# Denominators, scalings and the low halves of O: from VectorE to GpSimd

## The chip, the cores and the metric

The kernel runs on one core of one Trainium2 chip. The metric is the device time of one execution in microseconds. A core has five engines that work side by side, each in the order of its own queue: TensorE (PE, with its weight loads as PEld), VectorE (DVE), ScalarE (ACT), GpSimd (POOL) and SyncE (SP), which here issues the DMAs.

## The reference

Two attention branches A and B of the same form read the same x (2048 tokens, 640 channels, 32 heads of 20 channels); their outputs are mixed by a gate of each token. Each branch goes through four segments of 512 tokens with a memory M and its normalizer z:

```
for s in range(4):                      # qs, ks, vs: this segment's 512 tokens
    logits = qs @ ks.T * 20**-0.5 + mask          # mask: -1e9 where key > query
    a_dot  = softmax(logits) @ vs
    num    = phi(qs) @ M                           # phi(t) = t+1 if t>0 else exp(t)
    den    = phi(qs) @ z + 1e-6
    o      = g * num / den + (1 - g) * a_dot       # g = sigmoid(beta), one per head
    M, z   = M + phi(ks).T @ vs, z + phi(ks).sum
branch = concat(o) @ wo
out = gate * branch_A + (1 - gate) * branch_B      # gate = sigmoid(sum(x * gate_w))
```

(The mask of the reference is `ar[:, None] < ar[None, :]`, so a query sees the keys up to its own place.)

## The kernel before

The work is cut into eight batches t = 0..7: branch t % 2 of segment t // 2. A batch has eight groups u of four heads each; i = 8 t + u counts the 64 groups.

Products of x with the weights, and of O with wo, are done in three parts: each operand is split into hi (rounded by ScalarE) and lo (the difference). The lo halves of the weights come from GpSimd (`stage`, L541 and L516, 128x640, in four early cases from VectorE), those of O from `o_turn` (L948). Most matmuls use one half of the array, 64 rows of weights, so that two streams of them run side by side.

For each group the kernel makes the scores twice. The S units (L1240) give the scores with a query to a partition; VectorE adds the mask `tri` and takes each row's maximum in one operation (L1227, on a PSUM bank). The maxima are split and turned and sent into the rows of `qst`, so that the T units (L1330) give the scores turned and with their maximum taken off. ScalarE takes the exponential (L1322), GpSimd clears what lies past the diagonal (L1323), and TensorE multiplies with v in `pv_unit` (L1352), four heads at once, with a column of ones that gives the softmax's denominator.

What `pv_unit` and `mem_unit` (L827: phi(q) with M and z) leave in a PSUM bank goes through `weighed`. There are 112 calls: 64 for the attention (`which` = 0) and 48 for the memory (`which` = 1; the two batches of the first segment have no memory):

1. VectorE turns the bank in blocks of 32 (L934), after which each partition is a token and the denominators stand in column DH = 20 of each head.
2. `weight` makes the 16 factors of each partition: denominator times 1 / gate, then the reciprocal (L856). The product is L855 for the attention and L852 for the memory, where 1e-6 is added in the same instruction. Both run on VectorE, with both operands (the turned tile and the gates `gq`) in SBUF.
3. `pair` multiplies the 20 columns of each head by their factor (L878 into the tiles Z of the batch, L881 in place) and, where both attention and memory exist, adds the two (L886). `anyof` gives each of these to VectorE or GpSimd, to whichever has the smaller load.

When a Z tile has all its parts, `o_turn` turns it back (L952, 40 tiles in all), ScalarE makes hi (L947) and VectorE or GpSimd makes lo (L948). The q and k products (80 of them) are emptied by `hi_lo_out` and `hi_lo_phi` (L686 to L719).

The order of every engine's queue is written beforehand, by a planner inside the program. `put(engine, duration, instruction, then, prio)` puts a piece of work into a queue by priority, with a duration that stands in the code; the planner's clock goes on with the matmuls that it lays down, and an event `then` releases the next piece. What is written in this way is fixed when the kernel is built: on the chip each engine works its queue from front to back, and waits where an operand isn't there. The table `RULES` sets, for each of the 64 groups, in what succession S and T units are laid among the other products, how long the group's stretch is, and at which load of VectorE small units are held back. A line of it reads "order, span, calm, lag, room".

The names that count below: `fw` is the tile of 16 factors, `gqd` and `gqm` are the gates for attention and memory, `row` are the 42 large SBUF tiles that are used for everything, `mx` the row maxima, `bank` the eight PSUM banks.

Of the kernel before, what the change touches and what calls it, by code (L numbers as in the profile page):

```python
# [12 lines left out]
F32 = mybir.dt.float32  # L13
# [24 lines left out]
def r32(ap):  # L38
    return ap.bitcast(F32)
# [3 lines left out]
def tile_gated_mix_infini_attn(  # L43
# [44 lines left out]


    RULES = {  # L90
        0: "TTSTSTSTSS 1.0 2.63 0.33 6",
        1: "TSTSTSTSTS 1.0 2.38 0.46 6",
        2: "TSTTSSTSTS 1.0 2.38 0.46 4",
        3: "TSTTSSTSTS 1.0 2.38 0.42 4",
        4: "TTSSTTSSTS 1.0 2.93 0.42 4",
        5: "TSTTSSTSTS 0.996 2.28 0.34 6",
        6: "TSTTSSTSTS 0.954 2.96 0.46 8",
        7: "TSTTSSTSTS 0.964 2.58 0.34 8",
        8: "TSTSTSTSTS 1.0 2.21 0.33 8",
        9: "TTSTSTSTSS 0.95 2.38 0.36 6",  # L100
        10: "TSTSTSTSTS 1.0 2.12 0.46 6",
        11: "SSSTSTSTTT 1.0 2.12 0.46 3",
        12: "TSTTSSTSTS 1.021 2.11 0.33 4",
        13: "TSTSTSTSTS 1.0 2.38 0.33 6",
        14: "TSSTTSSTTS 1.025 2.36 0.36 6",
        15: "STSTSTSTST 1.067 2.36 0.36 6",
        16: "TSTSTSTSTS 1.029 2.38 0.33 6",
        17: "SSSTSTSTTT 1.029 1.79 0.33 6",
        18: "STTSSTTSST 1.029 2.14 0.46 6",
        19: "TSTSTSTSTS 1.0 1.84 0.31 6",  # L110
        20: "SSTSTSTSTT 1.0 1.84 0.31 6",
        21: "TSTSTSTSTS 1.0 2.38 0.36 6",
        22: "TTSTSTSTSS 1.0 2.38 0.33 6",
        23: "TTTSTSTSSS 1.012 2.38 0.33 3",
        24: "TSTSTSTSTS 0.989 2.38 0.42 4",
        25: "TTTSTSTSSS 0.993 2.38 0.33 6",
        26: "STSTSTSTST 0.989 2.38 0.33 6",
        27: "SSTSTSTSTT 0.96 3.85 0.46 6",
        28: "SSSTSTSTTT 0.922 3.85 0.46 6",
        29: "TSTSTSTSTS 0.987 2.38 0.34 6",  # L120
        30: "SSSTSTSTTT 1.014 2.38 0.36 6",
        31: "TSTTSSTSTS 1.08 2.38 0.36 6",
        32: "TTSTSTSTSS 1.0 1.82 0.36 6",
        33: "TTSSTTSSTS 1.0 2.38 0.33 6",
        34: "TSTSTSTSTS 1.0 2.38 0.34 6",
        35: "TTTSTSTSSS 1.0 1.93 0.34 6",
        36: "TTSTSTSTSS 1.033 2.93 0.33 4",
        37: "STTSSTTSST 0.932 1.97 0.33 6",
        38: "TSTSTSTSTS 1.0 2.74 0.33 6",
        39: "TSTSTSTSTS 0.971 2.38 0.31 6",  # L130
        40: "TSTSTSTSTS 1.005 2.38 0.32 6",
        41: "TSTSTTSTSS 1.007 2.38 0.32 6",
        42: "TSTSTTSTSS 1.039 2.38 0.32 6",
        43: "SSTSTSTSTT 1.039 2.38 0.34 6",
        44: "TSTSTSTSTS 1.032 2.73 0.33 8",
        46: "TSTTSSTSTS 1.032 2.73 0.31 8",
        47: "TSTSTSTSTS 0.953 1.56 0.3 6",
        48: "SSTSTSTSTT 0.953 1.56 0.46 6",
        49: "SSTSTSTSTT 0.915 1.56 0.36 6",
        50: "SSTSTSTSTT 0.915 1.56 0.42 6",  # L140
        51: "TSTSTSTSTS 0.991 2.93 0.33 6",
        52: "TSTSTSTSTS 1.0 1.87 0.33 6",
        54: "TSTSTSTSTS 0.992 2.38 0.33 6",
        55: "TTSTSTSTSS 1.0 2.38 0.33 6",
        56: "TSTSTSTSTS 1.0 2.38 0.33 6",
        58: "STSTSTSTST 1.0 3.17 0.33 3",
        59: "TSTSTSTSTS 1.055 3.17 0.33 8",
        60: "TSTTSSTSTS 0.988 2.38 0.36 6",
        61: "TSTSTSTSTS 0.976 2.38 0.33 6",
    }  # L150
    rule = {}
    DONE = {"A": 0.14, "D": 0.12, "G": 0.1, "S": 0.0}
# [33 lines left out]
    def put(e, dur, emit, then=None, prio=5, more=0.0):  # L186
        heapq.heappush(ready[e], (prio, next(seq), dur, emit, then, more))
        load[e] += dur
        start_next(e)
# [14 lines left out]
    def anyof(prio, then, **ways):  # L204

        e = min(ways, key=lambda e: load[e] + ways[e][0] + FAVOUR * (e == "D"))
        put(e, *ways[e], then, prio)
# [636 lines left out]
    def weighed(t, u, b, z, which):  # L844

        z4 = z.rearrange("p (a e) -> p a e", e=32)
        first = which == 1 or t < 2

        def weight():
            w = sb.tile([P, 16], F32, tag="fw", name=f"fw{which}_{t}_{u}", bufs=4)  # L850
            if which:
                nc.vector.scalar_tensor_tensor(  # L852
                    out=w, in0=z4[:, :, DH], scalar=1e-6, in1=gq[t][1][:, u, :], op0=ALU.add, op1=ALU.mult)
            else:
                nc.vector.tensor_tensor(out=w, in0=z4[:, :, DH], in1=gq[t][0][:, u, :], op=ALU.mult)  # L855
            nc.vector.reciprocal(w, w)  # L856
            return w

        def places(fn):
            todo = [k for k, _, _ in ZP[u] if (t, k) not in Z]  # L860
            left = then_all(len(todo) + 1, fn)
            for k in todo:
                Z[t, k] = None
                z_left[t, k] = (1 if t < 2 else 2) * sum(k == k2 for p in ZP for k2, _, _ in p)
                big.want((F32,), lambda tile, k=k: (Z.__setitem__((t, k), tile), left()), prio=1)
            left()

        def when_placed(fn):
            if all(Z[t, k] is not None for k, _, _ in ZP[u]):
                fn()  # L870
            else:
                at(clk[0] + 0.2, lambda: when_placed(fn))

        def scale(e, w):
            wb = w[:, :, None].to_broadcast([P, 16, DH])
            for k, e0, e1 in ZP[u]:
                dst = Z[t, k].rearrange("p (a e) -> p a e", e=32)[:, :, DH * u + e0 - 32 * k:DH * u + e1 - 32 * k]
                e.tensor_tensor(out=dst, in0=z4[:, :, e0:e1], in1=wb[:, :, e0:e1], op=ALU.mult)  # L878

        def scale_own(e, w):  # L880
            e.tensor_tensor(out=z4[:, :, :DH], in0=z4[:, :, :DH], in1=w[:, :, None].to_broadcast([P, 16, DH]), op=ALU.mult)  # L881

        def add(e):
            for k, e0, e1 in ZP[u]:
                dst = Z[t, k].rearrange("p (a e) -> p a e", e=32)[:, :, DH * u + e0 - 32 * k:DH * u + e1 - 32 * k]
                e.tensor_tensor(out=dst, in0=dst, in1=z4[:, :, e0:e1], op=ALU.add)  # L886

        def end():
            big.give(z)
            if which:  # L890
                mem_done.add((t, u))
            else:
                fin_done.add(i8)
                if all(8 * t + j in fin_done for j in range(8)):
                    gq_store.give(gq.pop(t))
            for k, _, _ in ZP[u]:
                z_left[t, k] -= 1
                if not z_left[t, k]:
                    big.want((F32,), lambda o, k=k: o_turn(t, k, o), prio=2)

        i8 = 8 * t + u
        n = len(ZP[u])
        D1, G1 = 0.11 * n + 0.42, 0.14 * n + 0.55

        def turned():
            bank.give(b)
            when_gates(lambda: put("D", 0.39, lambda: got_w.append(weight()), lambda: when_placed(go), prio=2))

        def when_gates(fn):
            if t in gq:  # L910
                fn()
            else:
                at(clk[0] + 0.2, lambda: when_gates(fn))

        got_w = []

        def go():
            w = got_w[0]
            if first:
                pair(D1, G1, lambda e: scale(e, w), end, 3)  # L920
            else:
                pair(0.56, 0.69, lambda e: scale_own(e, w), plus, 3)

        def plus():
            if (t, u) in mem_done:
                pair(D1, G1, add, end, 3)
            else:
                at(clk[0] + 0.2, plus)

        def pair(d, g, fn, then, prio):  # L930
            anyof(prio, then, D=(d, lambda: fn(nc.vector)), G=(g, lambda: fn(nc.gpsimd)))

        places(lambda: None)
        put("D", 0.635, lambda: nc.vector.transpose(out=z, in_=b), turned, prio=2)  # L934

    def o_turn(t, k, o):

        def turned():
            big.give(Z.pop((t, k)))
            big.want((F32R, F32R), halves, prio=2)  # L940

        def halves(hi, lo):
            def end():
                big.give(o)
                OTs[t, k] = (hi, lo)

            put("A", 0.535, lambda: nc.scalar.copy(hi, o), lambda: anyof(  # L947
                2, end, **{x: (c, lambda e=e: e.tensor_tensor(out=lo, in0=o, in1=r32(hi), op=ALU.subtract))  # L948
                           for x, c, e in (("D", 0.78, nc.vector), ("G", 1.255, nc.gpsimd))}), prio=2)

        z = Z[t, k]
        put("D", 0.63, lambda: nc.vector.transpose(out=o, in_=z), turned, prio=2)  # L952
# [676 lines left out]
```

## Time and profile before

| what | value |
|---|---|
| median of three runs | 1041.88 us (1040.1 to 1042.78) |
| the profiled execution | 1042.72 us, of which 1040.7 us lie between first and last instruction |
| TensorE clock granted | 0.998 on the mean |
| instructions | 29678 |
| busy, share of the span | PE 98%, PEld 81%, VectorE 79%, GpSimd 68%, ScalarE 60% |
| DMA | 217.65 MB, mean 209 GB/s |

A group in the profile is a line with engine, operation, tiles out<-in and shape; then the count, the busy time in us, the mean of one in ns, and the idle time of the engine just before these instructions with what ended it. The chain that ended last goes back from the last instruction, at each step to what released it or to the instruction before it on its engine. A wait is read "who <- for whom: us in total, times, longest".

### The profile page before, as it was taken

What the parts mean: (1) busy time and instruction counts of PE and PEld (TensorE: products, weight loads), DVE (VectorE), ACT (ScalarE), POOL (GpSimd) and SP (SyncE); (2) the same over time, 40 slices, a digit from 0 to 9 for tenths busy, and PEclk for the clock granted to TensorE, in tenths of its full rate; (3) what the DMA queues carried; (4) which work ended last, traced back from release to release, by engine and by line L of the source; (5) the groups of instructions that cost most, each with busy time, mean ns of one, the idle gap of its engine ahead of it and who ended that gap; (6) DMA issues with size and microseconds to landing.
All of it is one profiled execution on the core that took longest, in us unless ns stands there. A gap on an engine that the chain in (4) does not pass through costs nothing.

```text
span 1040.7 us, 29678 instructions
## 1 busy us (share of the span) xinstructions
PE 1023.1 (98%) x10610; PEld 843.0 (81%) x10610; DVE 824.3 (79%) x2814; ACT 629.1 (60%) x1286; POOL 703.1 (68%) x1230
## 2 busy tenths in 40 slices
PE   9999999999999999999999999999999999999998
PEld 7888787887888778888787888888778888687885
DVE  5797999768787789886979769987687966988864
ACT  6276667566565566665865556566575655666672
POOL 6266757667476686866857667686786766767584
PEclk9999999999999999999999999999999999999999
DMA  8998999758456677755856667675576666758631
GB/s 269 292 305 260 305 306 326 209 164 248 136 187 197 178 251 207 237 154 168 256 152 183 192 179 238 205 231 167 164 229 181 220 190 192 240 170 237 160 119 62
DMA packets 138595, 217.65 MB, mean 209 GB/s; under 512 B 12816, under 2 KB 48912, under 8 KB 138384
## 3 DMA queue, kind: packets, MB, share of 16 engines
q1 hardware_dynamic: 138448, 215.76, 68.1%
q8 instruction: 84, 1.38, 0.6%
q14 instruction: 63, 0.52, 0.2%
HBM read 141.26 MB, written 83.23 MB: 216 GB/s over the span
## 4 chain that ended last, share of the span: by engine, by line
PE 80%; DVE 9%; DMA 5%; ACT 2%; issue 2%; POOL 1%; SPq 0%; DVEq 0%; ACTq 0%
PE bank L734 47%; PE bank L1352 12%; PE bank L1330 7%; PE bank L1240 7%; PE bank L827 3%; PE bank L997 2%; DVE bank L1227 2%; DMA kst<-kd 1%; DVE row L934 1%; DVE row L703 1%; DMA qst<-qd 1%; DMA wst<-in_a_wk_dram 1%; PE bank L958 1%; DMA row<-in_xT_dram 1%; DMA kd<-row 0%
## 5 line engine op out<-in xcount | busy, mean ns | idle before, releaser
L1227 DVE CUSTOM_DVE_ANT_0 bank<-bank,tri 128x384 f32<-128x384 f32 (+3 forms) x1024 | 473.7, 514 | 77.6 <-PE bank L1240 60.6
L734 PE MATMUL bank<-row,wh 64*128 64x512 f32 x2308 | 520.6, 405 | 0.1
L1322 ACT ACTIVATE p<-bank 128x512 f32<-128x512 f32 x540 | 296.4, 602 | 160.2 <-PE bank L1330 123.9
L734 PEld LDWEIGHTS bank<-row,wh 64*128 64x128 f32 x2308 | 325.3, 186 | 19.2 <-PE bank L734 2.5
L734 PE MATMUL bank<-row,wl 64*128 64x512 f32 x1154 | 303.2, 400 | 0.0
L1323 POOL TENSOR_SCALAR_AFFINE_SELECT p<-p 128x256 f32<-128x256 f32 (+1 forms) x540 | 200.7, 383 | 102.8 <-ACT p L1322 95.0
L541 POOL TENSOR_TENSOR wl<-wst,wh 128x640 fp32r<-128x640 f32 x115 | 180.2, 1570 | 36.5 <-ACT wh L539 36.0
L734 PE MATMUL bank<-wvh,row 64*128 64x320 f32 x1280 | 194.4, 315 | 0.1
L1240 PE MATMUL bank<-kst,qst 60*128 60x384 f32 (+3 forms) x1024 | 181.0, 325 | 5.7 <-DVE mx L1227 2.4
L734 PEld LDWEIGHTS bank<-row,wl 64*128 64x128 f32 x1154 | 175.8, 185 | 6.8 <-issue 1.0
L1330 PE MATMUL bank<-qst,kst 62*128 62x384 f32 (+3 forms) x1024 | 177.6, 324 | 2.7 <-DVE row L693 1.2
L734 PEld LDWEIGHTS bank<-wvh,row 64*128 64x128 f32 x1280 | 159.6, 185 | 5.3 <-PE bank L734 1.1
L1240 PEld LDWEIGHTS bank<-kst,qst 60*128 60x128 f32 x1024 | 129.8, 186 | 21.8 <-DVE mx L1227 6.1
L1227 DVE DVE_READ_ACCUMULATOR2_ANT mx<- 128x1 f32 x1024 | 143.2, 140 | 0.1
L1330 PEld LDWEIGHTS bank<-qst,kst 62*128 62x128 f32 x1024 | 127.7, 185 | 18.0 <-issue 4.0
L934 DVE STREAM_TRANSPOSE row<-bank 128x512 f32<-128x512 f32 x112 | 77.9, 705 | 74.9 <-PE bank L1352 52.2
L1352 PE MATMUL bank<-p,vst 128*32 128x128 f32 (+3 forms) x1824 | 137.1, 421 | 0.0
L1352 PEld LDWEIGHTS bank<-p,vst 128*32 128x32 f32 x1824 | 56.6, 110 | 82.8 <-issue 57.4
L734 PE MATMUL bank<-wvl,row 64*128 64x320 f32 x640 | 110.6, 314 | 0.0
L539 ACT CAST wh<-wst 128x640 fp32r<-128x640 f32 x119 | 86.0, 738 | 32.9 <-PE bank L734 17.1
L734 PEld LDWEIGHTS bank<-wvl,row 64*128 64x128 f32 x640 | 87.8, 186 | 0.7 <-issue 0.2
L827 PE MATMUL bank<-row,mall 64*128 64x512 f32 x192 | 84.0, 606 | 1.1 <-DVE mx L1227 1.0
(99 smaller groups left out, 1296.8 us busy)
## 6 DMA issues: line engine op xcount, KB each, us to landing
qd<-row SPq DMA_DIRECT2D x120, 256.0 KB
kd<-row SPq DMA_DIRECT2D x120, 256.0 KB
qst<-qd SPq DMA_DIRECT2D x128, 240.0 KB
kst<-kd SPq DMA_DIRECT2D x128, 240.0 KB
wst<-wop SPq DMA_DIRECT2D x40, 320.0 KB
wst<-in_a_wq_dram SPq DMA_DIRECT2D x20, 320.0 KB
wst<-in_a_wk_dram SPq DMA_DIRECT2D x20, 320.0 KB
wst<-in_b_wq_dram SPq DMA_DIRECT2D x20, 320.0 KB
```

Source lines behind the costliest of these rows:

```text
L539: put("A", 0.628, lambda: nc.scalar.copy(wh, w3), lambda: put(lo_eng, lo_cost, lambda: lo.tensor_tensor(out=wl, in0=w3, in1=r32(wh), op=AL ...
L541: lambda: lo.tensor_tensor(out=wl, in0=w3, in1=r32(wh), op=ALU.subtract), end, prio=3), prio=6)
L734: return nc.tensor.matmul(bank_of, lhsT=w[ROWS[half]], rhs=x_[ROWS[half]], start=start, stop=stop)
L827: return nc.tensor.matmul(b, lhsT=w[r], rhs=r32(pqTs[t, half_m[half]][r, :]), start=start, stop=stop)
L934: put("D", 0.635, lambda: nc.vector.transpose(out=z, in_=b), turned, prio=2)
L997: return nc.tensor.matmul(b[:, :nh * E1], lhsT=r32(pkn[ROWS[half], P * n:P * (n + 1)]), rhs=vst[ROWS[half], n, LO[m] * E1:(HI[m] + 1) * E1 ...
L1227: put("D", w / 960.0 + 0.112, lambda: nc.vector.tensor_tensor_reduce(out=sc[:, off:off + w], in0=sc[:, off:off + w], in1=tri[:, L - w:], s ...
L1240: lane_ops[half].append((cost_r(w), lambda pair=pair, qb=qb, off=off, w=w, r=r, sc=sc: nc.tensor.matmul(sc[:, off:off + w], lhsT=q[r, pair ...
L1322: put("A", 0.493, lambda: nc.scalar.activation(pt, sc, AF.Exp, scale=SCALE), lambda: (bank.give(sc), put("G", 0.137 + 0.118 * len(todo), l ...
L1323: "G", 0.137 + 0.118 * len(todo), lambda: nc.gpsimd.affine_select(out=blocks, in_=blocks, pattern=[[0, len(todo)], [1, P]], base=0, channe ...
L1330: lane_ops[half].append((cost_r(w), lambda pair=pair, kb=kb, off=off, w=w, r=r, sc=sc: nc.tensor.matmul(sc[:, off:off + w], lhsT=k[r, pair ...
L1352: nc.tensor.matmul(po[32 * j:32 * j + 32, P * kb:], lhsT=vst[:, kb, h * E1:h * E1 + 32], rhs=pts[i, n, f][0][:, off:off + w], start=(kb == ...
```

## The change

In `weighed`, the product of denominators and gates is put to GpSimd for all 112 calls; for the 48 of the memory ScalarE first adds 1e-6 into `fw`. The reciprocal stays on VectorE and is released by GpSimd's product. `pair` (scaling and adding) and the lo halves of O go to GpSimd always. `fw` gets eight buffers in place of four. The table `RULES` has other entries for nearly all groups; its form and the code that reads it are as before.

```diff
     RULES = {
-        0: "TTSTSTSTSS 1.0 2.63 0.33 6",
+        0: "TSTSTSTSTS 1.001 3.28 0.33 6",
...
         def weight():
-            w = sb.tile([P, 16], F32, tag="fw", name=f"fw{which}_{t}_{u}", bufs=4)
+            w = sb.tile([P, 16], F32, tag="fw", name=f"fw{which}_{t}_{u}", bufs=8)
+            got_w.append(w)
+
+            def gated(den):
+                put("G", 0.19, lambda: nc.gpsimd.tensor_tensor(out=w, in0=den, in1=gq[t][which][:, u, :], op=ALU.mult), lambda: put(
+                    "D", 0.18, lambda: nc.vector.reciprocal(w, w), lambda: when_placed(go), prio=2), prio=1)
+
             if which:
-                nc.vector.scalar_tensor_tensor(
-                    out=w, in0=z4[:, :, DH], scalar=1e-6, in1=gq[t][1][:, u, :], op0=ALU.add, op1=ALU.mult)
+                put("A", 0.11, lambda: nc.scalar.add(w, z4[:, :, DH], 1e-6), lambda: gated(w), prio=1)
             else:
-                nc.vector.tensor_tensor(out=w, in0=z4[:, :, DH], in1=gq[t][0][:, u, :], op=ALU.mult)
-            nc.vector.reciprocal(w, w)
-            return w
+                gated(z4[:, :, DH])
...
         def turned():
             bank.give(b)
-            when_gates(lambda: put("D", 0.39, lambda: got_w.append(weight()), lambda: when_placed(go), prio=2))
+            when_gates(weight)
...
         def pair(d, g, fn, then, prio):
-            anyof(prio, then, D=(d, lambda: fn(nc.vector)), G=(g, lambda: fn(nc.gpsimd)))
+            put("G", g, lambda: fn(nc.gpsimd), then, prio)
...
-            put("A", 0.535, lambda: nc.scalar.copy(hi, o), lambda: anyof(
-                2, end, **{x: (c, lambda e=e: e.tensor_tensor(out=lo, in0=o, in1=r32(hi), op=ALU.subtract))
-                           for x, c, e in (("D", 0.78, nc.vector), ("G", 1.255, nc.gpsimd))}), prio=2)
+            put("A", 0.535, lambda: nc.scalar.copy(hi, o), lambda: put(
+                "G", 1.255, lambda: nc.gpsimd.tensor_tensor(out=lo, in0=o, in1=r32(hi), op=ALU.subtract), end, prio=2), prio=2)
```

In the order of the built programs the instructions of each kind are as many as before, apart from these: on VectorE 112 products, 23 scalings, 3 additions and 6 differences are gone, and GpSimd has these 144 more (1379 rows in place of 1235); ScalarE has 48 more. (One q or k product is emptied in the other of its two ways.) TensorE and SyncE have the same work in another succession. Three lines fewer stand in the table, so that the line numbers are smaller by one to four: the maxima are L1226, the products L851, the reciprocals L852, the weight splits L538 and L513, the turning of Z L951.

The first place is the fifth batch (t = 4), its second memory group, on VectorE before. `ISA` with `bank,tri` is the sum with mask and the maximum of a row; `ISA` with `mx` alone reads the maximum out.

```order
L934 STREAM_TRANSPOSE row37_9834_8212<-bank6_121 128x512
L1227 ISA bank3_118,mx31_8152<-bank3_118,tri_69 128x128
L1227 ISA mx31_8152 128x1
L852 SCALAR_TENSOR_TENSOR fw1_4_1_8227<-row37_9834_8212,gqm0_139 128x16
L856 RECIPROCAL fw1_4_1_8227<-fw1_4_1_8227 128x16
L703 TENSOR_TENSOR row41_9843_8216<-bank4_119,row16_9842_8215 128x512
L1227 ISA bank2_117,mx31_8152<-bank2_117,tri_69 128x128
```

The same group on VectorE now:

```order
L934 STREAM_TRANSPOSE row41_10191_8350<-bank5_120 128x512
L690 SCALAR_TENSOR_TENSOR row7_10143_8321<-bank4_119,row7_10143_8321 128x512
L934 STREAM_TRANSPOSE row22_10197_8352<-bank2_117 128x512
L852 RECIPROCAL fw1_4_1_8362<-fw1_4_1_8362 128x16
L1226 ISA bank0_115,mx31_8112<-bank0_115,tri_69 128x512
L1226 ISA mx31_8112 128x1
L934 STREAM_TRANSPOSE row40_10239_8385<-bank6_121 128x512
L852 RECIPROCAL fw1_4_2_8377<-fw1_4_2_8377 128x16
```

And on GpSimd now, where the product of the group stands:

```order
L538 TENSOR_TENSOR wl2_132<-wst1_124,wh2_131 128x640
L948 TENSOR_TENSOR row16_10176_8340<-row0_10157_8327,row13_10175_8339 128x512
L851 TENSOR_TENSOR fw1_4_1_8362<-fw1_4_1_8362,gqm0_139 128x16
L878 TENSOR_TENSOR row21_10070_8259<-row41_10191_8350,fw1_4_1_8362 128x16x12
L878 TENSOR_TENSOR row3_10193_8351<-row41_10191_8350,fw1_4_1_8362 128x16x8
L851 TENSOR_TENSOR fw1_4_2_8377<-fw1_4_2_8377,gqm0_139 128x16
L538 TENSOR_TENSOR wl1_130<-wst0_123,wh1_129 128x640
```

The product has left VectorE's queue, and the reciprocal there, which stands ahead of a row maximum, depends on a queue of GpSimd in which a weight split and a lo half of O come first.

The second place is the end of the kernel, the last group (fw0_7_7). VectorE before:

```order
L952 STREAM_TRANSPOSE row34_19729_16369<-row22_18361_15241 128x512
L934 STREAM_TRANSPOSE row28_19743_16391<-bank0_115 128x512
L855 TENSOR_TENSOR fw0_7_7_16400<-row28_19743_16391,gqd1_140 128x16
L856 RECIPROCAL fw0_7_7_16400<-fw0_7_7_16400 128x16
L881 TENSOR_TENSOR row28_19743_16391<-row28_19743_16391,fw0_7_7_16400 128x16x20
L952 STREAM_TRANSPOSE row27_19761_16421<-row20_18711_15537 128x512
```

GpSimd now:

```order
L1322 AFFINE_SELECT p4_20167_16357<-p4_20167_16357 128x2x128
L948 TENSOR_TENSOR row2_20216_16397<-row13_20201_16385,row36_20215_16396 128x512
L538 TENSOR_TENSOR wl3_134<-wst1_124,wh3_133 128x640
L851 TENSOR_TENSOR fw0_7_7_16444<-row18_20254_16436,gqd1_140 128x16
L881 TENSOR_TENSOR row18_20254_16436<-row18_20254_16436,fw0_7_7_16444 128x16x20
L886 TENSOR_TENSOR row9_19106_15494<-row9_19106_15494,row18_20254_16436 128x16x20
```

The last product and the last scaling stand on GpSimd, behind a lo half of O and a weight split.

More of the change, by code (lines that the diff above doesn't have):

```diff
@@ L90, in tile_gated_mix_infini_attn @@
     RULES = {
-        0: "TTSTSTSTSS 1.0 2.63 0.33 6",
[L92 to L149, printed above, removed]
+        0: "TSTSTSTSTS 1.001 3.28 0.33 6",
@@ new lines, in tile_gated_mix_infini_attn @@
+        2: "SSTSTSTSTT 1.0 2.38 0.33 6",
+        3: "TSTSTSTSTS 0.982 2.66 0.31 6",
+        4: "TSTTSSTSTS 0.971 1.95 0.33 6",
+        5: "TSSTTSSTTS 0.971 1.95 0.32 6",
+        6: "TSSTTSSTTS 1.0 2.38 0.33 6",
+        7: "STTSSTTSST 1.0 1.51 0.33 6",
+        8: "TTSSTTSSTS 1.02 1.52 0.31 3",
+        9: "SSSTSTSTTT 1.0 2.38 0.31 3",
+        11: "TSTSTTSTSS 0.957 2.38 0.32 8",
+        12: "TSTSTSTSTS 0.957 1.75 0.32 8",
+        13: "TSSTTSSTTS 1.003 2.38 0.42 6",
+        14: "TTSSTTSSTS 1.0 2.38 0.33 6",
@@ new lines, in tile_gated_mix_infini_attn @@
+        15: "STSTSTSTST 1.0 2.38 0.46 6",
+        16: "TSTSTSTSTS 1.0 2.38 0.46 8",
+        17: "SSTSTSTSTT 1.019 2.38 0.33 6",
+        18: "STSTSTSTST 1.0 1.98 0.33 6",
+        19: "STTSSTTSST 1.042 1.98 0.33 6",
+        20: "TSTSTSTSTS 0.982 2.22 0.46 6",
+        21: "TSTTSSTSTS 0.982 2.94 0.46 6",
+        22: "TSTSTSTSTS 1.0 2.0 0.33 6",
+        23: "SSTSTSTSTT 1.0 2.62 0.32 6",
+        24: "TSTSTTSTSS 1.0 2.62 0.32 6",
+        25: "TSTSTTSTSS 0.972 2.62 0.46 6",
+        27: "TSTSTSTSTS 1.051 2.38 0.3 3",
@@ new lines, in tile_gated_mix_infini_attn @@
+        28: "SSTSTSTSTT 1.0 2.38 0.33 6",
+        29: "TSTSTTSTSS 0.99 2.86 0.33 6",
+        30: "STTSSTTSST 0.99 2.86 0.38 3",
+        31: "TSTTSSTSTS 0.972 2.61 0.33 6",
+        32: "TSTSTSTSTS 1.0 2.38 0.33 6",
+        33: "TSTSTSTSTS 0.972 2.38 0.33 4",
+        34: "TSTTSSTSTS 1.022 1.5 0.46 6",
+        35: "TSTSTTSTSS 1.03 1.5 0.3 4",
+        36: "TSTSTSTSTS 1.034 3.14 0.33 6",
+        37: "TSTSTTSTSS 1.025 2.38 0.33 6",
+        38: "TSTSTSTSTS 0.951 2.38 0.33 6",
+        39: "TSTSTSTSTS 1.0 2.38 0.42 6",
@@ new lines, in tile_gated_mix_infini_attn @@
+        40: "TSTTSSTSTS 1.0 2.31 0.33 6",
+        41: "STTSSTTSST 1.026 2.31 0.36 6",
+        42: "TSTSTSTSTS 0.959 1.22 0.33 6",
+        43: "TTTSTSTSSS 0.959 1.31 0.3 6",
+        44: "TSSTTSSTTS 1.0 2.9 0.33 6",
+        45: "SSTSTSTSTT 1.0 2.36 0.33 6",
+        46: "SSTSTSTSTT 1.0 1.0 0.32 6",
+        47: "TSTSTSTSTS 0.964 2.38 0.33 6",
+        48: "TSTSTSTSTS 1.0 2.33 0.33 6",
+        49: "TTSTSTSTSS 1.02 3.17 0.33 6",
+        50: "TTSTSTSTSS 1.02 3.17 0.46 6",
+        51: "TTSTSTSTSS 1.02 3.27 0.32 6",
@@ L150, in tile_gated_mix_infini_attn @@
+        52: "TSTSTSTSTS 1.037 1.97 0.33 6",
+        53: "TTSSTTSSTS 0.969 3.01 0.31 3",
+        54: "TSTSTSTSTS 0.962 2.38 0.34 6",
+        56: "SSTSTSTSTT 0.951 2.2 0.34 6",
+        57: "TSTSTSTSTS 1.0 2.38 0.38 6",
+        58: "TSTSTSTSTS 1.019 1.34 0.38 6",
+        60: "TSTSTSTSTS 1.03 2.38 0.33 8",
     }
```

## The prediction

> **What bounds the kernel now.** I read the page first (busy times and the chain that ended last), then the busy time by stretches.
>
> ```profile
> PE 1023.1 (98%) x10610; PEld 843.0 (81%) x10610; DVE 824.3 (79%) x2814; ACT 629.1 (60%) x1286; POOL 703.1 (68%) x1230
> ...
> PE 80%; DVE 9%; DMA 5%; ACT 2%; issue 2%; POOL 1%; SPq 0%; DVEq 0%; ACTq 0%
> ```
>
> ```profile
> 80.00:500.00 420.00, 416.35 (x4451) 347.12 (x4444) 340.30 (x1176) 261.40 (x539) 286.43 (x505) 1.00 0.72 221
> 500.00:1000.00 500.00, 494.96 (x5157) 405.27 (x5155) 401.58 (x1389) 303.93 (x624) 351.58 (x620) 1.00 0.66 196
> ```
>
> The columns after the length are PE, PEld, DVE, ACT and POOL. TensorE is busy all but 8.7 of the 920 us between 80 and 1000, at full clock, so the matmuls bound the kernel. But almost all of them work on one half of the array, and "busy" is the union of both halves: one half can wait without any idle time in this row. The chain says as much: only 80% of it is TensorE's, and 9% (0.09 x 1040.7 = 94 us) is VectorE's, which is 94 / 824.3 = 11% of VectorE's busy time. GpSimd has 1% (10.4 us, 1.5% of its busy time), ScalarE 2% (20.8 us, 3.3% of its).
>
> What VectorE's part looks like shows best at 510 us, in the timeline, at one of the operations that the change moves:
>
> ```profile
> 509.85 1.56 POOL L541 TENSOR_TENSOR wl<-wst,wh 128x640 fp32r<-128x640 f32 x1
> ...
> 509.94 1.49 DVE L852 SCALAR_TENSOR_TENSOR fw<-row,gqm 128x16 f32<-128x16 f32 x1
> ...
> 511.47 0.25 DVE L856 RECIPROCAL fw<-fw 128x16 f32<-128x16 f32 x1
> 511.64 0.63 DVE L703 TENSOR_TENSOR row<-bank,row 128x512 fp32r<-128x512 f32 x1
> ...
> 512.19 0.28 DVE L1227 CUSTOM_DVE_ANT_0 bank<-bank,tri 128x128 f32<-128x128 f32 x1
> ...
> 512.58 0.18 PEld L827 LDWEIGHTS bank<-row,mall 64*128 64x128 f32 x1 [1.18 <-DVE mx L1227]
> ```
>
> Sixteen columns took 1.49 us, and they ended at 511.43, just when GpSimd's split of a weight tile ended (509.85 + 1.56 = 511.41). The row maximum (L1227) stood behind it in VectorE's queue, and TensorE's weight load waited 1.18 us for that maximum. Operations with two operands in SBUF do this; the reciprocal between them, with one, does not (0.25).
>
> The Trainium skill, "SBUF — State Buffer", section "Who interferes with whom", has this as a rule: VectorE with two SBUF inputs and a GpSimd instruction that reads SBUF share one read interface, and whichever came second is blocked until the first is through. The trace agrees (1.49 us, ended by the 1.56 us split). By that rule every such wait goes with the change; by the rows alone I count only what lies above the unblocked time, which comes to the same sum below.
>
> **Part 1: what leaves VectorE.** Groups by line and form (busy us, mean ns), and for some the shortest, median and longest of one:
>
> ```profile
> L855 DVE TENSOR_TENSOR fw<-row,gqd 128x16 f32<-128x16 f32 x64 | 22.4, 350 | 0.7
> ...
> L852 DVE SCALAR_TENSOR_TENSOR fw<-row,gqm 128x16 f32<-128x16 f32 x48 | 13.4, 279 | 0.2
> ...
> L881 DVE TENSOR_TENSOR row<-row,fw 128x320 f32<-128x320 f32 x8 | 6.3, 794 | 0.1
> ...
> L878 DVE TENSOR_TENSOR row<-row,fw 128x320 f32<-128x320 f32 x7 | 5.7, 813 | 0.1
> ...
> L886 DVE TENSOR_TENSOR row<-row,row 128x320 f32<-128x320 f32 x3 | 2.8, 930 | 0.1
> L878 DVE TENSOR_TENSOR row<-row,fw 128x256 f32<-128x256 f32 x3 | 2.7, 891 | 0.0
> ...
> L878 DVE TENSOR_TENSOR row<-row,fw 128x64 f32<-128x64 f32 x3 | 2.0, 661 | 0.0
> ```
>
> ```profile
> L855 DVE TENSOR_TENSOR fw<-row,gqd x64: 160/184/1517, 70.9 to 1026.0; 128x16 f32<-128x16 f32 x64
> ...
> L852 DVE SCALAR_TENSOR_TENSOR fw<-row,gqm x48: 109/160/1494, 250.1 to 973.5; 128x16 f32<-128x16 f32 x48
> ...
> L881 DVE TENSOR_TENSOR row<-row,fw x8: 490/618/1797, 427.2 to 1027.2; 128x320 f32<-128x320 f32 x8
> ...
> L878 DVE TENSOR_TENSOR row<-row,fw x15: 304/519/1516, 110.4 to 825.3; 128x320 f32<-128x320 f32 x7, 128x64 f32<-128x64 f32 x3, 128x256 f32<-128x256 f32 x3, 128x192 f32<-128x192 f32 x1
> ...
> L856 DVE RECIPROCAL fw<-fw x112: 252/253/255, 72.1 to 1026.9; 128x16 f32<-128x16 f32 x112
> ...
> L948 DVE TENSOR_TENSOR row<-row,row x6: 681/805/1652, 114.8 to 642.4; 128x512 fp32r<-128x512 f32 x6
> ```
>
> Busy time that leaves: 22.4 + 13.4 + 6.3 + 5.7 + 2.8 + 2.7 + 2.0, about 1.5 for the two L878 forms left out, and about 5.6 for the six L948 (6 x 0.94, between their median and longest) = 62 us, 7.6% of VectorE's work. Of it, blocked time above the median or the shortest of the same shape: L855 64 x (350 - 184) = 10.6; L852 48 x (279 - 160) = 5.7; L881 8 x (794 - 490) = 2.4; L878 7 x (813 - 490) + 3 x (891 - 490) + 3 x (661 - 304) = 4.5; L886 3 x (930 - 490) = 1.3; L948 6 x (940 - 681) = 1.6. Together 26 us blocked and 36 us of plain work.
>
> How much of each lay on the path? The plain work goes at VectorE's average, 11%: 36 x 0.11 = 4 us (from 0, if other work fills the place, to twice that). Blocked time comes unannounced in an order written beforehand, so it weighs more. The chain in order of time holds 19 pieces of the moved operations; the first, the large ones and the last are:
>
> ```profile
> 71.02 1.02 DVE fw L855
> ...
> 110.36 1.33 DVE row L878 x2
> ...
> 510.08 1.37 DVE fw L852
> ...
> 775.56 1.14 DVE fw L852
> ...
> 894.20 1.39 DVE fw L855
> ...
> 901.33 0.86 DVE fw L852
> ...
> 903.39 0.08 DVE fw L852
> ```
>
> The six large pieces make 7.1 us, so at least 0.27 of the 26 lies on the chain. The ends are 11% (3 us, the average) and 92% (1.37 of the 1.49 at 510 us; 24 us). I take 0.4, near the counted pieces and a little above for the small ones: 10.4 us.
>
> **Part 2: what GpSimd and ScalarE get.** The nearest rows of the same kind:
>
> ```profile
> L881 POOL TENSOR_TENSOR row<-row,fw 128x320 f32<-128x320 f32 x40 | 29.2, 730 | 37.6 <-DVE fw L856 36.2 <-PE bank L1330 1.4
> ...
> L878 POOL TENSOR_TENSOR row<-row,fw 128x320 f32<-128x320 f32 x25 | 18.5, 741 | 10.7 <-DVE fw L856 8.8 <-DVE fw L852 2.0
> L886 POOL TENSOR_TENSOR row<-row,row 128x320 f32<-128x320 f32 x21 | 18.3, 870 | 2.6 <-DVE row L881 2.3
> ...
> L948 POOL TENSOR_TENSOR row<-row,row 128x512 fp32r<-128x512 f32 x34 | 44.1, 1298 | 21.4 <-ACT row L947 21.1
> ...
> L1252 POOL TENSOR_TENSOR mt<-mx,mt 128x16 fp32r<-128x16 f32 x64 | 15.7, 245 | 29.7 <-ACT mt L1251 29.5
> ...
> L1251 ACT CAST mt<-mx 128x16 fp32r<-128x16 f32 x64 | 13.4, 210 | 34.9 <-DVE mx L1227 34.7
> ```
>
> 112 products of denominators and gates at 0.245 = 27; 8 x 0.730 + 15 x 0.741 at most + 3 x 0.870 + 6 x 1.298 = 27. GpSimd goes from 703 to 757 us (73%), and at its 1.5% this costs 0.8 us. ScalarE gets 48 additions of 1e-6 at 0.21 = 10 us; at 3.3%, 0.3 us. The moved scalings are slower by 0.24 each (730 against 490), but what follows them (adding, turning, splitting O) is wanted a batch later, and no wait of TensorE in the trace names them.
>
> **Part 3: the new wait.** The reciprocal stays on VectorE and now waits for GpSimd's product. If that is late, the row maxima behind the reciprocal are late too. Before, the trace has no such wait; it has two like it:
>
> ```profile
> DVE row L703 <- ACT row L691: 16.5, 22, 3.4
> ...
> DVE row L952 <- POOL row L886: 3.5, 3, 1.7
> ```
>
> Spread over all 80 of L703 and all 40 of L952 these are 0.21 and 0.09 us per operation; the ends for 112 reciprocals are 0 and 0.45 us (twice the worse row, since a product can stand behind a 1.56 us split). GpSimd's hand-over is the nearer kind, so I take 0.1: 11 us of VectorE, unannounced like the blocked time, so x 0.4 = 4.5 us back (0 to 20).
>
> **Part 4: the end.** Here the waits meet:
>
> ```profile
> 1025.55 1.29 POOL L948 TENSOR_TENSOR row<-row,row 128x512 fp32r<-128x512 f32 x1 [2.25 <-ACT row L947]
> ...
> 1026.04 0.83 DVE L855 TENSOR_TENSOR fw<-row,gqd 128x16 f32<-128x16 f32 x1
> ```
>
> The product of the last group was blocked for 0.65 us (0.83 against 0.18), hidden behind matmuls. In the new order it stands on GpSimd behind that L948 and behind a weight split whose lo half the early matmuls want right after the last attention product. Hidden or not: 0 to 2.8 us (both instructions); I take 1.
>
> **Sum.** -10.4 - 4 + 0.8 + 0.3 + 4.5 + 1 = -7.8 us. The new table of places writes the whole order anew and has no price in the trace; I give it 0, with 5 either way. Against the profiled execution (1042.72, with 1040.7 of it span) this is 1034.9; that execution lies 0.84 above the median of the runs, 1041.88, and from the median it is 1034.1. I forecast 1034.
>
> **The rivals.**
> 1. *The reciprocals block VectorE.* By the same terms without part 3 the gain is 12.3; part 3 gives 112 x 0.4 = 45 us back per us of mean wait, so from 0.27 us on the kernel is no faster. For it: GpSimd works in order with 1.56 us splits, and in the new order one of them stands directly ahead of the product in 25 of 112 places; against: GpSimd's own times hardly scatter, so an order that plans them can hold. At 0.45 us: -12.3 + 20 = +8, about 1050.
> 2. *Nothing to tell.* The waits of a half of the array go to whatever is late next (a bank that ScalarE still reads, a DMA, 5% of the chain): part 1's price is the low end, 3 + 0, less 2 for parts 2 and 4 and 1 or so for part 3: about 1042. The union's 99% speaks for it, the 1.18 us weight load against.
> 3. *GpSimd still holds VectorE up.* The Trainium skill, "Perfetto Trace Analysis", section "Optimizing Scalar/DVE Operations", warns that moving work between these two engines might not help, since they share a port. As a mechanism of this kernel: 55 us more of GpSimd would block whatever VectorE keeps. But what it keeps in the steady state reads at most one tensor from SBUF, apart from the few token gates, and all 112 reciprocals took 252 to 255 ns, whatever GpSimd did; so 1041, no gain, with a small chance.
>
> That the move doesn't take place is excluded: in the order no product, scaling or addition of these lines is left on VectorE.
>
> **How the numbers follow.** A measurement of this kernel tells about 0.3%, 3 us. The forecast has 0.63 (own range 1027 to 1040; it holds the faster cases), rival 1 has 0.19, rival 2 0.14, rival 3 0.04. Faster 0.63, same 0.18, slower 0.19. The range reaches down to 1022 (blocked time at 0.7 instead of 0.4, no new wait) and up to 1046, where a part of rival 1 is left out.
>
> **What would show it.** In the new profile: VectorE near 762 us busy, no operation on it with 16 columns over 0.3 us, GpSimd near 757, ScalarE near 639; VectorE's share of the chain below 9%; waits "DVE fw <- POOL fw" of about 11 us in total. I am wrong if those waits pass 30 us, if row maxima wait behind them, or if VectorE's share falls and DMA or ScalarE takes it over one for one.

## The result, and the profile after

The changed kernel takes 1030.53 us (median of 4 runs, 1028.84 to 1031.61) against 1041.37 of the kernel before: ratio 0.9894, 95% interval 0.9874 to 0.9914, so 10.8 us or 1.1% faster. The forecast was 1034. (All ratios here, and the time of experiment 1, are formed over the undisturbed runs; one execution of experiment 1 took 3420.65 us.)

The page of the changed kernel, busy times and chain:

```profile
PE 1012.2 (98%) x10610; PEld 842.2 (82%) x10610; DVE 772.2 (75%) x2671; ACT 637.0 (62%) x1333; POOL 744.5 (72%) x1374
...
PE 77%; DMA 9%; DVE 6%; ACT 2%; POOL 2%; issue 2%; SPq 1%; DVEq 0%; POOLq 0%; ACTq 0%
```

VectorE has 52 us less, GpSimd 41 more, ScalarE 8 more. VectorE's share of the chain fell from 9% to 6%, and DMA's rose from 5% to 9%. The stretches (PE, PEld, DVE, ACT, POOL):

```profile
80.00:500.00 420.00, 417.19 (x4521) 350.18 (x4519) 320.40 (x1127) 272.26 (x571) 310.75 (x576) 1.00 0.74 226
500.00:1000.00 500.00, 495.14 (x5198) 409.30 (x5196) 380.20 (x1335) 312.46 (x660) 375.77 (x708) 1.00 0.65 194
```

TensorE's busy time hardly differs (912.3 of 920 us against 911.3), but 9719 matmuls fall into these stretches instead of 9608. So the halves of the array must wait less, which the union of their busy times cannot show.

The operations that moved, by line and form, and the wait that is new:

```profile
L852 DVE RECIPROCAL fw<-fw 128x16 f32<-128x16 f32 x112 | 26.9, 245 | 10.6 <-POOL fw L851 10.1
...
L851 POOL TENSOR_TENSOR fw<-row,gqd 128x16 f32<-128x16 f32 x64 | 14.5, 227 | 60.1 <-DVE row L934 57.7 <-DMA kst<-kd 2.1
...
L855 ACT ACTIVATE fw<-row 128x16 f32<-128x16 f32 x48 | 11.1, 232 | 22.9 <-DVE row L934 22.8
L851 POOL TENSOR_TENSOR fw<-fw,gqm 128x16 f32<-128x16 f32 x48 | 10.7, 225 | 11.6 <-ACT fw L855 11.2
```

```profile
DVE fw L852 <- POOL fw L851: 10.1, 22, 1.3
```

On GpSimd the products take 225 to 227 ns each. The reciprocals waited for them 10.1 us in all, in 22 of 112 cases.

### The profile page after: what moved, and what is told of

It is laid out like the page before. It is cut to its first block, busy times and chain, and to the rows that moved or that the text cites. A ratio compares the mean times of both kernels' runs of the same rounds, so it can differ in the third digit from the quotient of the medians.

```text
span 1029.4 us, 29770 instructions
## 1 busy us (share of the span) xinstructions
PE 1012.2 (98%) x10610; PEld 842.2 (82%) x10610; DVE 772.2 (75%) x2671; ACT 637.0 (62%) x1333; POOL 744.5 (72%) x1374
## 4 chain that ended last, share of the span: by engine, by line
PE 77%; DMA 9%; DVE 6%; ACT 2%; POOL 2%; issue 2%; SPq 1%; DVEq 0%; POOLq 0%; ACTq 0%
PE bank L731 45%; PE bank L1351 12%; PE bank L1329 6%; PE bank L1239 6%; PE bank L824 3%; PE bank L996 2%; DVE bank L1226 2%; DMA kd<-row 2%; DMA wst<-in_x_dram 1%; DVE pgt L623 1%; DMA lin<-nat 1%; DMA qd<-row 1%; DMA wst<-in_a_wk_dram 1%; PE bank L957 1%; DMA wop<-lin 1%
## 5 line engine op out<-in xcount | busy, mean ns | idle before, releaser
L1226 DVE CUSTOM_DVE_ANT_0 bank<-bank,tri 128x384 f32<-128x384 f32 (+3 forms) x1024 | 473.9, 514 | 96.7 <-PE bank L1239 75.3
L1322 POOL TENSOR_SCALAR_AFFINE_SELECT p<-p 128x256 f32<-128x256 f32 (+1 forms) x536 | 195.5, 378 | 71.9 <-ACT p L1321 62.8
L538 POOL TENSOR_TENSOR wl<-wst,wh 128x640 fp32r<-128x640 f32 x115 | 180.2, 1569 | 29.6 <-ACT wh L536 28.4
L731 PE MATMUL bank<-wvh,row 64*128 64x320 f32 x1280 | 199.0, 321 | 0.0
L1226 DVE DVE_READ_ACCUMULATOR2_ANT mx<- 128x1 f32 x1024 | 143.5, 140 | 0.1
L1351 PE MATMUL bank<-p,vst 128*32 128x256 f32 (+3 forms) x1800 | 137.3, 422 | 0.0
L1321 ACT ACTIVATE row<-bank 128x512 f32<-128x512 f32 x104 | 56.5, 605 | 39.6 <-PE bank L1329 34.5
```

What stands on the lines that cost most here:

```text
L538: lambda: lo.tensor_tensor(out=wl, in0=w3, in1=r32(wh), op=ALU.subtract), end, prio=3), prio=6)
L731: return nc.tensor.matmul(bank_of, lhsT=w[ROWS[half]], rhs=x_[ROWS[half]], start=start, stop=stop)
L1226: put("D", w / 960.0 + 0.112, lambda: nc.vector.tensor_tensor_reduce(out=sc[:, off:off + w], in0=sc[:, off:off + w], in1=tri[:, L - w:], s ...
L1321: put("A", 0.493, lambda: nc.scalar.activation(pt, sc, AF.Exp, scale=SCALE), lambda: (bank.give(sc), put("G", 0.137 + 0.118 * len(todo), l ...
L1322: "G", 0.137 + 0.118 * len(todo), lambda: nc.gpsimd.affine_select(out=blocks, in_=blocks, pattern=[[0, len(todo)], [1, P]], base=0, channe ...
L1351: nc.tensor.matmul(po[32 * j:32 * j + 32, P * kb:], lhsT=vst[:, kb, h * E1:h * E1 + 32], rhs=pts[i, n, f][0][:, off:off + w], start=(kb == ...
```

## Experiments

**1. One operand instead of two, in the order of before.**

```diff
-                nc.vector.scalar_tensor_tensor(
-                    out=w, in0=z4[:, :, DH], scalar=1e-6, in1=gq[t][1][:, u, :], op0=ALU.add, op1=ALU.mult)
+                nc.vector.tensor_scalar(w, z4[:, :, DH], 1e-6, 1.0, op0=ALU.add, op1=ALU.mult)
...
-                nc.vector.tensor_tensor(out=w, in0=z4[:, :, DH], in1=gq[t][0][:, u, :], op=ALU.mult)
+                nc.vector.tensor_scalar(w, z4[:, :, DH], 0.0, 1.0, op0=ALU.add, op1=ALU.mult)
```

> The kernel before, every engine's order unchanged, but the 112 products of denominators and gates read one SBUF tensor only (the gates are left out: times 1.0). Port theory (the gain came from VectorE operations with two SBUF operands being blocked by GpSimd): none of the 112 takes over 0.3 us any more, their 16 us of blocked time go, and at the 0.4 of the prediction the time falls by 6.5 to about 1035. Table theory (the gain came from the new succession of units): stays at 1041 within 3. Load theory (the gain came from fewer operations on VectorE): stays at 1041, since the count is the same.

Measured: 1039.78 us, ratio 0.9995 (0.9979 to 1.0012). The edit failed to remove what it was meant to remove (shortest, median and longest of one, in ns):

```profile
L854 DVE TENSOR_SCALAR fw<-row x64: 153/176/1504, 70.3 to 1025.5; 128x16 f32<-128x16 f32 x64
L852 DVE TENSOR_SCALAR fw<-row x48: 109/157/1274, 251.0 to 973.0; 128x16 f32<-128x16 f32 x48
```

Sixteen columns of one SBUF tensor are held up just as long. With means of 358 and 253 ns, 64 x (358 - 176) + 48 x (253 - 157) ns = 16 us are blocked, as much as before. So the run says nothing for or against any theory, except that two operands are not the criterion; and leaving out the gates shows no gain by itself. It needed an operation that GpSimd had not held up so far; the reciprocals were one.

**2. A reciprocal in place of each product, in the order of before.** Both products are replaced by `nc.vector.reciprocal(w, z4[:, :, DH])`; the gates and the 1e-6 are left out.

> The kernel before with the same order everywhere; each of the 112 products on VectorE is replaced by a reciprocal of the denominator, followed by the reciprocal that was there (gates left out). A reciprocal was never held up by GpSimd so far (252 to 255 ns), a sum with one SBUF operand was. Port theory: no fw operation over 0.3 us; 16 us of blocked time go, 8 us of plain work come (64 x 0.07 + 48 x 0.09), so 1041 - 6.5 + 0.9 = about 1035. Table theory and load theory: 1041 or 1042.

Measured: 1035.47 us, ratio 0.9957 (0.9936 to 0.9978), 4.5 us faster. The longest of one, and one that runs beside a weight split of GpSimd:

```profile
L854 DVE RECIPROCAL fw<-row x64: 231/249/256, 70.7 to 1017.5; 128x16 f32<-128x16 f32 x64
L852 DVE RECIPROCAL fw<-row x48: 192/211/255, 249.4 to 965.0; 128x16 f32<-128x16 f32 x48
```

```profile
508.92 1.56 POOL L541 TENSOR_TENSOR wl<-wst,wh 128x640 fp32r<-128x640 f32 x1
...
509.07 0.25 DVE L852 RECIPROCAL fw<-row 128x16 f32<-128x16 f32 x1
```

This is the place that the prediction showed with 1.49 us: the same order, 0.15 us into the split, and now 0.25 us. With the number of operations and their places unchanged, the blocked time of the products was worth 4.5 us (2.3 to 6.7 by the interval), and VectorE's share of the chain went to 5%. Experiment 1 leaves out the gates as well and gained nothing, so it is not the missing operand. Port theory's cause, the blocked time, holds for the products, though its criterion of two operands does not; the two others had 1041 or 1042.

**3. The products back on VectorE, in the order of the changed kernel.** `nc.gpsimd` becomes `nc.vector` in the one line that multiplies; places, table and every other engine's order stay.

> The changed kernel with the same order of TensorE, ScalarE and SyncE and the same table; only the 112 products are issued on VectorE instead of GpSimd, at the same place of the succession. Port theory: blocked time comes back, 16 us or a little more since GpSimd is busier, 1036 to 1040. Table theory: 1030 to 1032. Load theory: 112 x 0.17 = 19 us more plain work at 11%, 2 us: about 1033.

Measured: 1035.46 us, ratio 0.9937 (0.9915 to 0.9959), so 4.5 us of the gain are gone.

```profile
L851 DVE TENSOR_TENSOR fw<-row,gqd 128x16 f32<-128x16 f32 x64 | 17.7, 276 | 0.6
L851 DVE TENSOR_TENSOR fw<-fw,gqm 128x16 f32<-128x16 f32 x48 | 14.8, 315 | 0.8 <-ACT fw L855 0.7
```

```profile
L851 DVE TENSOR_TENSOR fw<-row,gqd x64: 111/178/1445, 74.0 to 1019.7; 128x16 f32<-128x16 f32 x64
...
L851 DVE TENSOR_TENSOR fw<-fw,gqm x48: 111/171/1557, 248.4 to 965.1; 128x16 f32<-128x16 f32 x48
```

Their medians are 178 and 171 ns, so 64 x 0.098 + 48 x 0.144 = 13 us are blocked. The time lies half a microsecond below the port theory's range and above those of the others; by itself this run does not tell blocked time from load, which the next one does.

**4. The same, but with reciprocals.** On VectorE `nc.vector.reciprocal(w, den)` stands where GpSimd had the product; the gates are left out.

> The changed kernel with the same order otherwise; each product on GpSimd is replaced by a reciprocal of the denominator on VectorE at the same place (gates left out). VectorE has 112 more operations, 27 us, none of which GpSimd can hold up. Port theory: 27 x 0.11 = 3 us less what the hand-over to GpSimd cost (4.5): 1029 to 1032, clearly below the 1035.5 with products on VectorE. Load theory: 1034 to 1036, as with the products.

Measured: 1031.37 us, ratio 0.9909 (0.9887 to 0.9931), not to be told from the changed kernel (0.9894). None of the reciprocals was held up:

```profile
L851 DVE RECIPROCAL fw<-row x64: 194/250/255, 74.1 to 1016.2; 128x16 f32<-128x16 f32 x64
...
L851 DVE RECIPROCAL fw<-fw x48: 193/243/254, 249.7 to 961.6; 128x16 f32<-128x16 f32 x48
```

```profile
PE 1014.3 (98%) x10610; PEld 841.5 (82%) x10610; DVE 790.9 (77%) x2783; ACT 637.6 (62%) x1333; POOL 722.6 (70%) x1262
...
PE 83%; DMA 7%; DVE 6%; POOL 1%; ACT 1%; issue 1%; SPq 1%; POOLq 0%; ACTq 0%; DVEq 0%
```

VectorE has as many operations as in experiment 3 and is busy for 790.9 us (798.0 there), and yet the loss is not there. So the loss of experiment 3 points to blocked time and not to load: the time lies in port theory's range and outside that of load theory. The step is likely rather than certain by this pair alone, since the runs differ by 4.1 us in the medians and 2.9 in the ratios, and their intervals overlap from 0.9915 to 0.9931; experiment 2 shows the same in the order of before. Against the changed kernel the run measures one difference, 27 us of plain work on VectorE less the hand-over to GpSimd: 0.8 us by the medians, 1.6 by the ratios. So the hand-over costs no more than the work that it saves VectorE; what each costs alone, this run does not tell.

**5. Each table with the other code.** Only the entries of `RULES` are exchanged.

> The changed code with the table of the kernel before. Table theory: 1041 or worse. Port theory: the blocked time stays away, so below 1041 even with a table chosen for another order, 1032 to 1039.

> The code of before with the table of the changed kernel. Table theory: 1031. Port theory: 1041 or worse, up to 1050, since the blocked time stays and the table was chosen for another order.

Measured: the changed code with the table of before 1063.24 us, ratio 1.0207 (1.0177 to 1.0236); the code of before with the new table 1067.38 us, ratio 1.0250 (1.0218 to 1.0282). The table theory's "1041 or worse" holds the first, but gave no size, and missed the second; port theory missed both. Neither had foreseen 22 to 27 us of loss. Such a foreign table is worse than the plain one of experiment 6. A table is worth what it is only with the code that it was fitted to, and the question "table or code" cannot be asked by exchanging it.

**6. One line for all groups.**

```diff
     RULES = {
-        0: "TTSTSTSTSS 1.0 2.63 0.33 6",
...
+        0: "TSTSTSTSTS 1.0 2.38 0.33 6",
     }
```

> The code of before with a table of one line for all groups (TSTSTSTSTS 1.0 2.38 0.33 6). Both theories: slower than 1041 by 10 to 35, since no stretch is fitted. It is the base for the next kernel.

> The changed code with the same table of one line. Port theory: 5 to 12 us below the code of before with that table. Table theory: the same as the code of before with that table, within 3 us.

Measured: before 1054.87 us, ratio 1.0138 (1.0112 to 1.0165); changed code 1052.68 us, 1.0105 (1.0073 to 1.0137). The difference of 3.4 us has the sign of the port theory, less than its 5 to 12, and the intervals overlap: inconclusive. One possible reason for the smaller gain is in the waits of the changed code with the plain table, more than the 10.1 us of the fitted one:

```profile
DVE fw L797 <- POOL fw L796: 17.6, 33, 1.7
```

Another possible one is the granted clock: 0.995 on the mean of the four executions of the changed code against 0.998 for the code of before, and the one of the four that had 0.998 took 1048.09 us. How the time goes with the clock is seen on the kernel before: among its 50 executions beside the experiments, those at 0.997 took 1042.8 us on the mean and those at 1.000 took 1039.9, so about 1 us for each 0.001.

**7. The large operations alone.** In the order of before, the 32 scalings, additions and lo halves that VectorE had are issued on GpSimd at the same places.

```diff
-            anyof(prio, then, D=(d, lambda: fn(nc.vector)), G=(g, lambda: fn(nc.gpsimd)))
+            anyof(prio, then, D=(d, lambda: fn(nc.gpsimd)), G=(g, lambda: fn(nc.gpsimd)))
...
-                           for x, c, e in (("D", 0.78, nc.vector), ("G", 1.255, nc.gpsimd))}), prio=2)
+                           for x, c, e in (("D", 0.78, nc.gpsimd), ("G", 1.255, nc.gpsimd))}), prio=2)
```

> The kernel before, same places in the succession and same table, but the 32 large operations that the load rule had given to VectorE (23 scalings, 3 additions, 6 lo halves of O) are issued on GpSimd. Port theory: 10 us of blocked time and 16 us of plain work leave VectorE, 10 x 0.4 + 16 x 0.11 = 6, less 1 to 3 for 26 us that GpSimd's succession didn't allow for: 1036 to 1039. Table theory: 1041 or worse.

Measured: 1040.48 us, ratio 1.0003 (0.9990 to 1.0015): nothing gained, where port theory had 1036 to 1039. The page shows 21 us less on VectorE and what came instead, GpSimd's share of the chain at 4% (1% before):

```profile
PE 1021.4 (98%) x10610; PEld 844.2 (81%) x10610; DVE 803.7 (77%) x2782; ACT 628.3 (60%) x1286; POOL 722.0 (70%) x1262
...
PE 76%; DVE 7%; DMA 6%; POOL 4%; ACT 3%; issue 2%; SPq 1%; POOLq 0%; ACTq 0%; DVEq 0%
```

**8. Everything moved, in the order of before.** As in 7, and `weight` issues `nc.scalar.add` and `nc.gpsimd.tensor_tensor` where it had VectorE's products.

> The kernel before, same places and same table, with every engine as in the changed kernel: products and the 32 large operations on GpSimd, 1e-6 on ScalarE. So the move without a succession that knows of it. Port theory by the prediction's terms: -10.4 - 4 + 1 + 4.5 to 9 for reciprocals that wait for GpSimd: 1033 to 1038. Table theory: 1041 or worse. What lies between this and 1030.5 is the worth of the new succession.

Measured: 1046.76 us, ratio 1.0055 (1.0038 to 1.0072), slower than before. Port theory's 1033 to 1038 missed; the table theory's "1041 or worse" holds it. The reciprocals' row, and the chain:

```profile
L856 DVE RECIPROCAL fw<-fw 128x16 f32<-128x16 f32 x112 | 28.1, 252 | 51.6 <-POOL fw L853 25.6 <-POOL fw L855 25.1
```

```profile
PE 70%; POOL 9%; DVE 6%; DMA 6%; ACT 4%; issue 3%; SPq 1%; POOLq 0%; ACTq 0%; DVEq 0%
```

VectorE stood still for 50.7 us before its reciprocals, 0.45 us each, and GpSimd took 9% of the chain. Against experiment 7 only the products and their 1e-6 have moved, and the time is 5 us longer by the ratios. (`fw` still has four buffers here, and no wait for a free one shows.) This is rival 1 of the prediction, with the very wait that it had named.

**9. The fourth corner: the new order, with the engines of before.** As in 3, and VectorE also gets the scalings, additions and lo halves that the old load rule would have given it (45 here, 32 in the kernel before). The 48 additions of 1e-6 stay on ScalarE, so the engines are those of before but for these.

> The succession, the table and the planned places of the changed kernel, but the engines of the kernel before: products on VectorE, and of the scalings, additions and lo halves those for which the old load rule would have chosen VectorE (45 here), issued at the same places. It is the fourth corner beside before, after, and the order of before with everything moved (1046.8). Port theory: the 5 us of the products come back, and for the large operations 0 (as in the order of before) to 6: 1035 to 1041. Table theory: 1031.

Measured: 1048.18 us, ratio 1.0075 (1.0052 to 1.0098), beyond both expectations. The new order, which was laid out for the other engines, is no gain by itself; with the old engines in it, it is slower than the old order. Some 3 of the 8 us may be the clock, by the rate of experiment 6 (an estimate): it was granted 0.996 on the mean here, against 0.999 for the kernel before beside it. Against experiment 3 the 45 large operations cost 12.7 us, though in the old order the 32 there were worth nothing (7). The chain and the waits on the maxima:

```profile
PE 68%; DVE 9%; issue 2%; DMA 1%; ACT 1%; POOL 0%; SPq 0%; DVEq 0%; POOLq 0%; ACTq 0%
```

```profile
PEld bank L1241 <- DVE mx L1228: 10.5, 10, 2.3
PEld bank L1331 <- DVE mx L1228: 8.3, 17, 1.5
PE bank L1241 <- DVE mx L1228: 7.4, 7, 1.9
```

In the changed kernel the corresponding waits are 6.7, 3.4 and 4.2 us. (The chain of this run stops short of the start: its shares add up to 81%.)

**10. A better version.** The changed kernel still has small copies on VectorE, which spread the token gates. Their row, and what the chain makes of four of them at 666 us, in the changed kernel:

```profile
L623 DVE COPY pgt<-pg x64: 117/166/1575, 43.3 to 668.4; 32x4 f32<-32x4 f32 x64
```

```profile
666.04 0.37 DVE pgt L623
...
666.42 0.35 DVE pgt L623
...
666.78 1.57 DVE pgt L623
...
668.37 0.17 DVE pgt L623
```

```diff
-                nc.vector.tensor_copy(
+                nc.scalar.copy(
                     pgt[32 * j:32 * j + 32, 16 * s + a:16 * s + 16:4], pg[32 * a:32 * a + 32, NB * s:NB * (s + 1)])
```

> The changed kernel, the same order otherwise, but the 64 small copies of the token gates (32x4, VectorE, up to 1.58 us each beside GpSimd) are issued on ScalarE at the same places. Port theory: their 8 us of blocked time go from VectorE, of which most lies on the chain: 2 to 5 us faster, 1026 to 1029. Table theory and load theory: 1030 to 1031.

Measured: 1025.03 us, ratio to before 0.9851 (0.9826 to 0.9875), the fastest here, with the same order otherwise. That is 5.5 us below the changed kernel by the medians and 4.5 by the ratios, whose intervals just touch (0.9874 to 0.9914 there).

```profile
L623 ACT COPY pgt<-pg x64: 178/195/199, 41.8 to 664.0; 32x4 f32<-32x4 f32 x64
```

```profile
PE 83%; DMA 8%; DVE 2%; ACT 2%; issue 2%; POOL 1%; SPq 1%; DVEq 0%; ACTq 0%; POOLq 0%
```

ScalarE takes 195 ns for one, 199 at the longest; VectorE's share of the chain falls to 2%. It is a second edit that takes away blocked time and leaves the order, and it gained what was expected or a little more. It takes plain work off VectorE too, 11 of the 18.6 us that the copies had there, so by itself it does not part blocked time from load; load theory had 1030 to 1031.

## Why the prediction was right, point by point

- **What leaves VectorE:** 62 us were reckoned, 52 went. The token copies took 4.3 us more than before (18.6 for 14.3). Most of the rest is in the reckoning: durations of neighbours overlap (at 510 us the product "began" 0.14 us before its forerunner ended), so their sum is more than the busy time.
- **Blocked time at 0.4:** of the 26 us, 16 belong to the products, 6.5 us by the prediction. Experiment 2 has 4.5 (2.3 to 6.7) with 7 us more of plain work on VectorE (54.8 us for the three groups of `fw` against 64.1 less the 16 blocked); experiments 3 and 4, which differ in the blocked time above all, have 2.9 to 4.1 for 13 us. Shares of 0.28 and of 0.22 to 0.31: somewhat under 0.4, in both orders, within wide intervals. For the other 10 us, of the large operations, the term was too much: moving them alone gained nothing (7). As to the chain that the 0.4 was read from, the prediction called six pieces the large ones; two more of 0.85 us (L881 at 571.20, L948 at 642.57) are about as large as its smallest, 0.86.
- **Plain work at 11%, 4 us:** no run shows it by itself. In experiment 4, 27 us of additional plain work, less the hand-over to GpSimd, cost 0.8 us by the medians and 1.6 by the ratios, within the scatter; at 11% and with no hand-over it would be 3.
- **GpSimd and ScalarE:** 757 and 639 us forecast, 744.5 and 637.0 measured. A product takes 226 ns, not 245, which is 2 of the 12 us; here too durations of neighbours overlap.
- **The new wait:** 11 us forecast, 10.1 measured. Its price, 4.5 us, was not measured alone: by experiment 4 the hand-over costs no more than 27 us of plain work on VectorE do. So the size of the wait was right only because the order was made for it; without that (experiment 8) it is 50.7 us, rival 1's 0.45 us per reciprocal. Rival 1's 1050 is close to the 1046.8 measured.
- **The end, 1 us:** from the end of the last attention product to the last instruction there are 16.0 us now, 15.5 before, so 0.5. The weight split was over at 1013.38, before that product's end at 1013.41:

```profile
1011.82 1.56 POOL L538 TENSOR_TENSOR wl<-wst,wh 128x640 fp32r<-128x640 f32 x1
...
1014.35 0.23 POOL L851 TENSOR_TENSOR fw<-row,gqd 128x16 f32<-128x16 f32 x1 [0.97 <-DVE row L934]
```

- **The new succession at 0:** this is where the sum was mis-sized. It was treated as a term beside the others. The four corners show that it is none (the one below on the left with the two reservations of experiment 9):

| | engines of before | engines of the changed kernel |
|---|---|---|
| order of before | 1040 to 1041 | 1046.8 |
| new order | 1048.2 | 1030.5 |

Each alone costs 6 to 8 us, both together gain 10.8. Of these 10.8, 4.5 come with the products in the new order, most of it blocked time by experiments 3 and 4. The other 6 are what experiment 3 keeps, with the products on VectorE: they come from the large operations and the new order together; how much of them is blocked time and how much a closer succession was not separated, and stays open.
- **The sum:** that -7.8 came near the measured 10.8 us is in part luck. Blocked time (-10.4) was set high, for the products and, in the order of before, for the large operations; the price of the new wait (+4.5) pulled the other way; and what the new order and the large operations gain together, 6 us, had no term of its own.
- **Rival 2** (whatever is late next takes it): partly so; DMA's share of the chain rose from 5 to 9% while VectorE's fell from 9 to 6%. That is the prediction's own sign of being wrong, DMA taking it over one for one, and yet 10 us were left over. The sign was a poor one: experiment 4 takes as long as the changed kernel within the noise, and has 83% of its chain on TensorE and 7% on DMA, against 77% and 9%.
- **Rival 3** (GpSimd still holds VectorE up) was right in kind and wrong in size: with more on GpSimd the token copies went from 224 to 290 ns on the mean, and moving them was worth about 5 us. They read one SBUF tensor, so by the prediction's criterion of two they should not have been held up. The sentence of the Trainium skill, "Perfetto Trace Analysis", section "Optimizing Scalar/DVE Operations", that moving work between these engines might not help, fits the outcome of experiment 8 (1.0055), not that of the changed kernel (0.9894). It gives a shared port as the reason; in experiment 8 the wait that grew is that of reciprocals for GpSimd's results (50.7 us).

## What to carry to other kernels

A short operation in an in-order queue can cost part of what it waits, not only what it takes: look at the longest of a group, not at the mean, before judging an operation of 16 columns or 4 too small to matter. Where queues are laid out beforehand, moving an operation to another engine and laying out the queues again are one change; here the move without the new order lost time, and so did the new order without the move, where both together gained. To separate a blocked wait from load, put an operation of about the same length in the same place that the runs show not to be held up.

## What the runs showed of the hardware that was not expected

On VectorE a sum with a constant, of one SBUF tensor with 16 columns (median 157 to 176 ns), took up to 1504 ns, and a copy of 32x4 up to 1575, each until a weight split of GpSimd was through (they ended at 895.18 and 668.35 us of their runs, the splits at 895.14 and 668.32); reciprocals of the same tensors took 192 to 256 ns in all 224 cases of experiment 2. The prediction had put the line at two SBUF operands. The Trainium skill, "SBUF — State Buffer", section "Who interferes with whom", also counts copies and `tensor_scalar` among those that can take the shared ports, in their two-port modes. The runs agree that both can be held up (1504 and 1575 ns); in which mode they ran, no run shows.
